# Re-ordering the hand-written stretch between the last filter lags and the first feed-forward block of an S4 + SwiGLU kernel

## The chip, the cores and the metric

The kernel runs on one core of one Trainium2 chip. The metric is the device time of one execution in microseconds (us). Below, PE is TensorE (matmuls), DVE is VectorE, ACT is ScalarE, POOL is GpSimd and SP is SyncE, which only issues DMAs here.

## The reference

Two layers, each a state-space block (S4) and then a feed-forward block (SwiGLU), on one sequence of 2048 rows with 512 channels; both layers use the same parameters:

```python
x = A_u
x = x + _A_ref(_layernorm(x), A_re, A_im, B_re, B_im, C_re, C_im, log_dt, Dskip)
x = x + _B_ref(_layernorm(x), w_gate, w_up, w_down)
...                                      # the same two lines once more

def _A_ref(u, ...):
    P = jnp.exp(logdA[:, :, None] * l)                      # 512 x 128 x 2048
    K = jnp.einsum("dn,dnl,dn->dl", Cc, P, dB).real         # one filter per channel
    y = irfft(rfft(pad(u)) * rfft(pad(K)))[:L]              # long convolution
    return y + u * Dskip

def _B_ref(x, w_gate, w_up, w_down):
    return (_silu(x @ w_gate) * (x @ w_up)) @ w_down        # 512 -> 1376 -> 512
```

## The kernel before

**Stages.** The sequence is cut into four blocks of 512 rows. A first stage makes the filter: the 512 channels are taken in eight chunks of 64; for each, VectorE and ScalarE build powers, TensorE sums them to the filter's lags (`lags`, 128 matmuls) and transforms them (`products`) into spectra. The first of the four spectrum blocks stays in SBUF (`w0r`), the others go to DRAM (`wdr`). In between, the first two row blocks of the layer-normed input are transformed as well (`direct`, and for the second row block `second`) and go to DRAM (`udr`).

The second stage works through the eight pairs (layer, row block) in the order of `SEQ`: convolution (`ssm_half`, for either half of the channels in four frequency steps) and feed-forward (`ffn`). Convolution of a pair and feed-forward of the pair before it run side by side: TensorE does the feed-forward's matmuls, VectorE mostly the spectra's products.

**A convolution step** of row block b: for each k up to b, multiply the input spectrum of block b-k with filter spectrum k (`yk`, then `t` and an add: lines 781 and 784), two instructions that combine real and imaginary parts into `y` (786, 787), eight inverse-transform matmuls `pi` (803), and then `combine`: a copy by ScalarE for frequencies 0 and 1 (753), two VectorE additions for 3 and 2 (761, 762). For k > 0 the spectra `w` and `uu` come by DMA from DRAM (777, 779). After the four steps two more groups of VectorE instructions make the output rows (818 to 822 and 827 to 834).

**The stretch that the change re-orders** lies between the two stages, about 240 to 315 us into the run. There the order of ScalarE's, VectorE's, TensorE's and GpSimd's instructions is that of the program, written by hand as a list of generator steps: `take(g, n)` issues the next n pieces of generator g. SyncE's order, and everything after this list, is set by a planner that runs the program on its own clock, with priorities (`tc.high_priority`). In the list are:

- `lags` of the last channel chunk, `spread_in` (a copy of the lags, line 507), `spread_pe` (32 matmuls, line 523, and a copy into `kt`, 525), `skip` (the direct term's addition on GpSimd, 503);
- `conv[0]` and `conv[1]`: the two halves of the first row block's convolution; `block1`: the second row block's;
- `scales`: eleven small VectorE instructions (344 to 356) that make the weights' scale factors, after the last `largest` (339);
- `split(hi, lo, load)`: the feed-forward weights as two fp16 parts, high part by ScalarE (664, for the down projection 689), low part by VectorE (669, 692), and their loads (660, 683, 685);
- `direct_size`: the largest direct term (ScalarE 192, VectorE 193);
- `first_parts`, `odd`, `rest`: the remaining spectra (580 and 531, with ScalarE 598 and 599 and VectorE 600); `spectra(6)`, third step: VectorE 563;
- `norm`: layer norm of the first 256 rows for the feed-forward (203 to 209, 848, transposes 850, 853, 855);
- `second(*sec[-1])`: the last transform of the second row block's input (16 matmuls, line 296, and a copy, 299).

Tiles share buffers by tag: a tile gets a buffer of its tag when the earlier tile in it is done with. The tag `w` has three buffers, for the `y` of the first convolutions (`yf`) and for the spectra `w`; `uu` has three; the PSUM tag `sml` has four.

Of the kernel before, what the change touches and what calls it, by code (L numbers as in the profile page):

```python
# [74 lines left out]
def kernel(ctx, tc, x, a_re, a_im, b_re, b_im, c_re, c_im, log_dt, d_skip,  # L75
# [12 lines left out]
    def tl(shape, name, tag, dt=F32):  # L88
        return sb.tile(shape, dt, name=name, tag=tag, bufs=BUFS[tag])
# [4 lines left out]
    def psml(shape, name):  # L94
        return ps.tile(shape, F32, name=name, tag="sml", bufs=4)
# [89 lines left out]
    dsk, th32 = tdk[0:1, 0], tdk[:, 1]  # L185
    nc.sync.dma_start(dsk, d_skip)
    dmax = sb.tile([1, 1], F32, name="dmax")

    def direct_size():

        da = tl([1, D], "da", "sg")
        A.activation(da, dsk, AF.Abs)
        V.tensor_reduce(dmax, da, axis=AX.X, op=OP.max)


# [304 lines left out]
    def skip(ch, kt, eng):  # L500

        k = kt[0:1, :, 0]
        eng.tensor_tensor(k, k, dsk[:, ch * DC:(ch + 1) * DC].rearrange("p (g d) -> p g d", g=4), OP.add)

    def spread_in(pk):
        ks = tl([P, 4, 16, 16], "ks", "nn")
        A.activation(ks, pk.rearrange("p d (c a) -> p a c d", a=4), AF.Copy)
        return ks
# [120 lines left out]
    def take(it, n):  # L629
        for _ in range(n):  # L630
            next(it, None)
# [70 lines left out]
    def inputs():  # L702

        for layer, b in SEQ:
            if layer == 0 and b < 2:
                if b == 0:
                    nc.sync.dma_start(u4, udr[0][0, 0].rearrange("q p c i d -> p q c i d"))
                for h in range(2):
                    for i, q in enumerate(QORD):
                        if b == 0:  # L710
                            u = u4[:, q]
                            for qn in (QORD[:3], QORD[3:], (), ())[i] if h else ():
                                nc.sync.dma_start(u4[:, qn], udr[0][0, 1, qn])
                        else:
# [23 lines left out]
    def ssm_half(layer, b, h):  # L738
# [3 lines left out]
        bb = {}  # L742
        if half and not yl2:
            yl2.append(tl([P, 2, 2, 2, HD], "yl2", "hf", F16))
        if (layer, b) == SEQ[1] and not yf2:
            t = tl([P, 2, 2, HD], "yf2", "hf")
            yf2.extend((t[:, 0], t[:, 1]))

        def combine(q, pi):
            if q < 2:  # L750
                pair = tl([P, 2, 2, HD], "bb", "bd") if h == 0 or not first else bb1[:, q]
# [9 lines left out]
                V.tensor_tensor(bb[q], s, pi, OP.subtract)  # L761
                V.tensor_tensor(s, s, pi, OP.add)

        late = []
        for s in range(4):
            hq, q, u = ahead.pop(0)
            nxt = next(spec, None)
            if nxt:
                ahead.append(nxt)
            yk = tl([P, NQ, 2, 2, DC], "yk", "y1")  # L770
            y = yc if half else yf2[s % 2] if (layer, b) == SEQ[1] else tl([P, 2, HD], "yf", "w")
            for k in range(b + 1):
                if k == 0:
                    w, uu = w0r[:, h, q], u
                else:
                    w = tl([P, NQ, 2, DC], "w", "w")
                    nc.sync.dma_start(w, wdr[k, h, q])
                    uu = tl([P, NQ, 2, DC], "uu", "uu")
                    nc.sync.dma_start(uu, udr[layer][b - k, h, q])
                t = tl([P, NQ, 2, 2, DC], "t", "t") if k else yk  # L780
                V.tensor_tensor(t, uu.unsqueeze(2).to_broadcast([P, NQ, 2, 2, DC]),  # L781
                                w.unsqueeze(3).to_broadcast([P, NQ, 2, 2, DC]), OP.mult)
                if k:
                    V.tensor_tensor(yk, yk, t, OP.add)  # L784
            yo = whole(y)
            V.tensor_tensor(yo[:, 0], yk[:, :, 0, 0], yk[:, :, 1, 1], OP.subtract)
            V.tensor_tensor(yo[:, 1], yk[:, :, 0, 1], yk[:, :, 1, 0], OP.add)
            if (layer, b, h, s) == (0, 1, 0, 0):
                yield
# [4 lines left out]
            pi = psml([P, 2, HD], "pi")  # L794
            with tc.high_priority(offset=0 if first else BOOST):
                for o in range(2):
                    if half:
                        terms = [(eih[:, q, 0 if i == o else 1 + o, le], yl[:, ly, i])
                                 for i in range(2) for le, ly in ((0, 0), (0, 1), (1, 0))]
                    else:  # L800
                        terms = [(ei[:, q, 0 if i == o else 1 + o], y[:, i]) for i in range(2)]
                    for k, (e, m) in enumerate(terms):
                        PE.matmul(pi[:, o], lhsT=e, rhs=m, start=k == 0, stop=k == len(terms) - 1)  # L803
            late.append((q, pi))
            if first and q < 2 or len(late) > 1:
                combine(*late.pop(-1 if first and q < 2 else 0))
            yield
        for l in late:
            combine(*l)
# [148 lines left out]
    with tc.manual_schedule(engines={mybir.EngineType.Activation, mybir.EngineType.DVE, mybir.EngineType.PE, mybir.EngineType.Pool}):  # L958
# [59 lines left out]
        def later(make):  # L1018

            yield from make()  # L1020
# [35 lines left out]
        def use(c, t):  # L1056

            box, kt, n = {}, kt2[:, c % 2], starts[c + 1]

            def copy():  # L1060
                box["ks"] = spread_in(box["pk"])
                if c < NCH - 2:
                    spread(c, box["ks"], kt)
            at(t, lambda: box.update(pk=lags(ts[c], gs[c])))
            at(t + 7.1, copy)
            if c == NCH - 2:
                at(t + 10.0, lambda: spread_pe(box["ks"], kt))
# [14 lines left out]
        def weights(n, t0, t1, t2, t3):  # L1082
# [15 lines left out]
            if t3:  # L1098
                at(t3, largest)

        starts = [0.0, 31.0, 62.0] + [93.0 + 28.0 * k for k in range(NCH)]
        for i in range(NCH - 1):
            t = starts[i]
# [18 lines left out]

        c, kts, tail = NCH - 1, (kt2[:, 0], kt2[:, 1]), {}
# [16 lines left out]
        def split(hi, lo, load=0):  # L1142
            for _ in range(load):
                loads.pop(0)()
            for _ in range(hi):
                his.pop(0)()
            for _ in range(lo):
                los.pop(0)()
# [61 lines left out]
        split(1, 0)  # L1210
        take(odd, 1)
        take(norm, 1)
# [65 lines left out]
```

## Time and profile before

| | |
|---|---|
| time, median of 3 runs | 1153.27 us (1152.6 to 1155.06) |
| the profiled execution | 1153.04 us, its span 1151.2 us |
| TensorE clock granted in it, mean | 0.993 |
| busy, share of the span | PE 95%, DVE 87%, ACT 52%, POOL 9% |
| instructions | 24402 |

The profile gives for every instruction its engine, its line in the kernel, its start and its length. "Idle before" is the time for which an engine had nothing to do before an instruction, with the instruction that released it. The profiled execution is 1.84 us longer than its span.

### The profile page before, as it was taken

What the parts mean: (1) busy time and instruction counts of PE and PEld (TensorE: products, weight loads), DVE (VectorE), ACT (ScalarE), POOL (GpSimd) and SP (SyncE); (2) the same over time, 40 slices, a digit from 0 to 9 for tenths busy, and PEclk for the clock granted to TensorE, in tenths of its full rate; (3) what the DMA queues carried; (4) which work ended last, traced back from release to release, by engine and by line L of the source; (5) the groups of instructions that cost most, each with busy time, mean ns of one, the idle gap of its engine ahead of it and who ended that gap; (6) DMA issues with size and microseconds to landing.
All of it is one profiled execution on the core that took longest, in us unless ns stands there. A gap on an engine that the chain in (4) does not pass through costs nothing.

```text
span 1151.2 us, 24402 instructions
## 1 busy us (share of the span) xinstructions
PE 1096.6 (95%) x9942; PEld 874.8 (76%) x9942; DVE 998.7 (87%) x1585; ACT 598.9 (52%) x1198; POOL 108.9 (9%) x163
## 2 busy tenths in 40 slices
PE   2989999998899999999999999999999999999998
PEld 1868888887776868686868777877768687776874
DVE  8999999988999899998999999989994999973221
ACT  6989998834554453567443534655424352334211
POOL 0112222210000110011010000110000100000000
PEclk9989999999999999999999999999999999999999
DMA  5367777867583355332355444334443155302000
GB/s 210 128 166 166 162 182 174 187 187 264 167 268 108 100 153 192 116 96 70 119 139 133 135 140 143 111 116 117 136 136 126 51 134 155 106 29 48 14 24 19
DMA packets 127314, 150.38 MB, mean 131 GB/s; under 512 B 50897, under 2 KB 75985, under 8 KB 127202
## 3 DMA queue, kind: packets, MB, share of 16 engines
q1 hardware_dynamic: 115298, 123.32, 35.1%
q0 software_dynamic: 11904, 25.50, 9.7%
q8 instruction: 78, 1.28, 0.4%
q14 instruction: 34, 0.28, 0.1%
HBM read 98.70 MB, written 33.82 MB: 115 GB/s over the span
## 4 chain that ended last, share of the span: by engine, by line
PE 40%; DVE 21%; issue 7%; DMA 4%; ACT 2%; POOL 1%; SPq 1%; DVEq 0%; ACTq 0%; POOLq 0%
PE pgu L916 7%; PE pgu L917 7%; PE pgu L919 7%; PE py L931 4%; PE py L932 4%; PE py L933 4%; PE pi L803 4%; DVE t L781 3%; DVE yk L784 3%; PE pf L280 2%; DVE z L228 2%; DVE yk L781 2%; DMA mix<-nn 2%; DVE sg L923 1%; DVE hl L925 1%
## 5 line engine op out<-in xcount | busy, mean ns | idle before, releaser
L916 PE MATMUL pgu<-mix,wsl 128*128 128x256 f16 x1280 | 299.2, 273 | 2.9 <-DVE sg L923 2.8
L917 PE MATMUL pgu<-mix,wsl 128*128 128x256 f16 x1280 | 298.8, 273 | 0.0
L919 PE MATMUL pgu<-mix,wsl 128*128 128x256 f16 x1280 | 195.6, 273 | 0.0
L917 PEld LDWEIGHTS <-wsl 128*128 128x128 f16 x1280 | 125.4, 98 | 19.8 <-issue 3.4
L931 PE MATMUL py<-wsl,hh 128*128 128x512 f16 (+1 forms) x352 | 133.5, 379 | 4.9 <-DVE xg L936 3.2
L916 PEld LDWEIGHTS <-wsl 128*128 128x128 f16 x1280 | 125.4, 98 | 16.0
L919 PEld LDWEIGHTS <-wsl 128*128 128x128 f16 x1280 | 125.5, 98 | 14.9
L933 PE MATMUL py<-wsl,hl 128*128 128x512 f16 (+1 forms) x352 | 133.4, 379 | 0.2 <-DVE hl L925 0.2
L922 ACT ACTIVATE sg<-pgu,sc 128x512 f32<-128x512 f32 x80 | 54.6, 683 | 129.1 <-PE pgu L919 126.2
L932 PE MATMUL py<-wsl,hh 128*128 128x512 f16 x320 | 121.3, 379 | 0.0
L781 DVE TENSOR_TENSOR t<-uu,w 128x1024 f32<-128x1024 f32 x96 | 116.8, 1217 | 0.2
L784 DVE TENSOR_TENSOR yk<-yk,t 128x1024 f32<-128x1024 f32 x96 | 116.8, 1217 | 0.2
L923 DVE SCALAR_TENSOR_TENSOR sg<-pgu,sc,sg 128x512 f32<-128x512 f32 x80 | 59.6, 745 | 52.5 <-ACT sg L922 52.3
L531 PE MATMUL pw<-kt,ek 128*128 128x256 f32 (+1 forms) x384 | 91.3, 375 | 0.0
L924 ACT ACTIVATE hh<-sg 128x512 f16<-128x512 f32 x80 | 50.1, 627 | 78.1 <-DVE sg L923 78.1
L803 PE MATMUL pi<-yl,mix 128*128 128x256 f16 x576 | 78.9, 272 | 1.6 <-ACT yl L792 1.2
L531 PEld LDWEIGHTS pw<-kt,ek 128*128 128x128 f32 x384 | 73.0, 194 | 8.4
L280 PE MATMUL pf<-z,eh 128*128 128x256 f16 x576 | 74.9, 273 | 0.6 <-DVE z L228 0.6
L781 DVE TENSOR_TENSOR yk<-u,w0r 128x1024 f32<-128x1024 f32 x56 | 68.1, 1217 | 0.8 <-ACT u L282 0.8
L925 DVE TENSOR_TENSOR hl<-sg,hh 128x512 f16<-128x512 f32 x80 | 54.8, 685 | 15.5 <-ACT hh L924 15.4
L496 PE MATMUL pk<-re,g 128*32 128x64 f32 x1024 | 65.1, 317 | 2.8 <-DMA g<-g 1.9
L932 PEld LDWEIGHTS <-hh 128*128 128x128 f16 (+1 forms) x352 | 34.5, 98 | 41.7 <-issue 5.9
(238 smaller groups left out, 2159.1 us busy)
## 6 DMA issues: line engine op xcount, KB each, us to landing
uu<-udr SPq DMA_DIRECT2D x96, 256.0 KB, 3.0
w<-wdr SPq DMA_DIRECT2D x96, 256.0 KB, 2.7
udr<-u POOLq DMA_DIRECT2D x32, 256.0 KB, 2.6
g<-g POOLq DMA_DIRECT2D x6, 1024.0 KB, 9.1
udr<-u SPq DMA_DIRECT2D x16, 256.0 KB, 3.0
n<-xdr SPq DMA_DIRECT2D x4, 1024.0 KB, 5.6
kdr<-ks SPq DMA_DIRECT2D x6, 512.0 KB, 2.8
kt<-kdr SPq DMA_DIRECT2D x24, 128.0 KB, 3.0
```

What stands on the lines that cost most here:

```text
L280: PE.matmul(pf[:, o], lhsT=e, rhs=m, start=k == 0, stop=k == len(terms) - 1)
L531: PE.matmul(pw[:, i], lhsT=e, rhs=kt[:, :, c + 4 * k0:4 * k1:4, :].rearrange("p g k d -> p k g d"), start=c == 0, stop=c == 3)
L781: V.tensor_tensor(t, uu.unsqueeze(2).to_broadcast([P, NQ, 2, 2, DC]), w.unsqueeze(3).to_broadcast([P, NQ, 2, 2, DC]), OP.mult)
L784: V.tensor_tensor(yk, yk, t, OP.add)
L803: PE.matmul(pi[:, o], lhsT=e, rhs=m, start=k == 0, stop=k == len(terms) - 1)
L916: PE.matmul(o, lhsT=wgu(wi, k, 0)[:, fs], rhs=nh[:, k], start=k == 0, stop=False)
L917: PE.matmul(o, lhsT=wgu(wi, k, 1)[:, fs], rhs=nh[:, k], start=False, stop=False)
L919: PE.matmul(o, lhsT=wgu(wi, k, 0)[:, fs], rhs=nlo[:, k], start=False, stop=k == 3)
L923: V.scalar_tensor_tensor(sg, pgu[:, 1], sc6[:, 4:5], sg, OP.mult, OP.mult)
L931: PE.matmul(py[:, r], lhsT=hh[:n, f, rc], rhs=wd(f, 0)[:n], start=f == 0, stop=False)
L932: PE.matmul(py[:, r], lhsT=hh[:n, f, rc], rhs=wd(f, 1)[:n], start=False, stop=False)
L933: PE.matmul(py[:, r], lhsT=hl[:n, f, rc], rhs=wd(f, 0)[:n], start=False, stop=f == FT - 1)
```

## The change

The list of the hand-written stretch gets another order, and around it these lines change:

```diff
     def direct_size():
-        da = tl([1, D], "da", "sg")
+        both = tl([1, D + DC], "da", "sg")
+        da = both[:, :D]
+        dlast.append(both[:, D:])
+        A.activation(dlast[0], dsk[:, D - DC:], AF.Copy)
         A.activation(da, dsk, AF.Abs)
+        yield
         V.tensor_reduce(dmax, da, axis=AX.X, op=OP.max)
...
-            y = yc if half else yf2[s % 2] if (layer, b) == SEQ[1] else tl([P, 2, HD], "yf", "w")
+            y = yc if half else yf2[s % 2] if (layer, b, h + s > 0) == (*SEQ[1], True) else tl([P, 2, HD], "yf", "w")
...
+            if ahead_two and s == 0:
+                q, u = QORD[0], tl([P, NQ, 2, DC], "u", "u")
+                nc.sync.dma_start(u, udr[0][1, 0, q])
...
+            made.append((q, y, yl))
+            if ahead_two and s == 0:
+                yield
+                continue
+            while made:
+                if ahead_two and s == 1:
+                    yield
+                inverse(*made.pop(0))
...
+                if c == NCH - 2:
+                    tail["sp"] = sp
+                    ats = ats[:2]
```

`ahead_two` holds for layer 0, row block 1, first half; `inverse` is the old code of the eight `pi` matmuls and `combine`, now a function; the last lines take the third and fourth piece of `spectra(6)` out of the plan. The list itself (lines that stay are given where the order needs them):

```diff
+        take(conv[0], 1)
+        take(tail["sp"], 2)
+        while tops:
+            tops.pop(0)()
+        scales()
+        split(1, 0)
+        size = direct_size()
+        next(size)
         ks = spread_in(pk)
...
+        last = second(*sec[-1])
         take(conv[0], 1)
+        split(0, 1)
+        split(0, 0, 1)
+        take(size, 1)
         spread_pe(ks, kts[1])
         skip(c, kts[1], G)
         take(conv[0], 1)
-        while tops:
-            tops.pop(0)()
-        scales()
+        block1 = ssm(0, 1)
+        take(block1, 1)
+        first_parts(c, 0)
         split(1, 0)
-        first_parts(c, 0)
-        take(conv[0], 1)
-        split(1, 1)
-        split(0, 0, 1)
         first_parts(c - 1, 3)
         split(1, 0)
         take(conv[0], 1)
         first_parts(c - 1, 1)
         split(1, 0)
+        take(last, 2)
+        split(0, 1)
+        split(0, 0, 1)
         take(conv[1], 1)
         first_parts(c, 2)
         take(conv[1], 1)
-        split(0, 1)
-        split(0, 0, 1)
...
         take(odd, 2)
         take(conv[1], 1)
-        direct_size()
-        block1 = ssm(0, 1)
         take(norm, 1)
         take(rest, 2)
         take(odd, 1)
+        take(odd, 2)
         take(norm, 1)
         take(block1, 1)
         take(rest, 1)
-        take(odd, 2)
...
         sizes(c, kts[1], ks)
-        take(second(*sec[-1]), 2)
```

So the scale factors, the first high part and the largest direct term are issued ahead of the copy of the last lags; the first convolution step is issued ahead of the last spectrum's addition; the second row block's first two steps (VectorE's five instructions each, without their inverse transforms) come after the first convolution's third step and after the norm's second piece; the last transform of the second row block's input comes after the third `first_parts`. `skip` reads a copy of the last 64 direct terms; the tile with the originals shares its buffer with `t`, so a `t` now waits for `direct_size` alone. The `y` of that row block's first step takes a buffer of tag `w`.

More of the change, by code (lines that the diff above doesn't have):

```diff
@@ L187 @@
     dmax = sb.tile([1, 1], F32, name="dmax")
+    dlast = []
     def direct_size():
-        da = tl([1, D], "da", "sg")
+        both = tl([1, D + DC], "da", "sg")
+        da = both[:, :D]
+        dlast.append(both[:, D:])
+        A.activation(dlast[0], dsk[:, D - DC:], AF.Copy)
         A.activation(da, dsk, AF.Abs)
+        yield
         V.tensor_reduce(dmax, da, axis=AX.X, op=OP.max)
@@ L502, in skip @@
         k = kt[0:1, :, 0]
-        eng.tensor_tensor(k, k, dsk[:, ch * DC:(ch + 1) * DC].rearrange("p (g d) -> p g d", g=4), OP.add)
+        d = dlast[0] if ch == NCH - 1 else dsk[:, ch * DC:(ch + 1) * DC]
+        eng.tensor_tensor(k, k, d.rearrange("p (g d) -> p g d", g=4), OP.add)
     def spread_in(pk):
@@ L713, in inputs @@
                                 nc.sync.dma_start(u4[:, qn], udr[0][0, 1, qn])
+                        elif h + i == 0:
+                            continue
                         else:
@@ L744, in ssm_half @@
             yl2.append(tl([P, 2, 2, 2, HD], "yl2", "hf", F16))
-        if (layer, b) == SEQ[1] and not yf2:
-            t = tl([P, 2, 2, HD], "yf2", "hf")
-            yf2.extend((t[:, 0], t[:, 1]))
         def combine(q, pi):
@@ L762, in combine, with inverse @@
                 V.tensor_tensor(s, s, pi, OP.add)
-        late = []
-        for s in range(4):
[L766 to L769, printed above, removed]
+        late, made = [], []
+        ahead_two = (layer, b, h) == (0, 1, 0)
+        def inverse(q, y, yl):
+            pi = psml([P, 2, HD], "pi")
+            with tc.high_priority(offset=0 if first else BOOST):
+                for o in range(2):
+                    if half:
+                        terms = [(eih[:, q, 0 if i == o else 1 + o, le], yl[:, ly, i])
+                                 for i in range(2) for le, ly in ((0, 0), (0, 1), (1, 0))]
+                    else:
+                        terms = [(ei[:, q, 0 if i == o else 1 + o], y[:, i]) for i in range(2)]
+                    for k, (e, m) in enumerate(terms):
+                        PE.matmul(pi[:, o], lhsT=e, rhs=m, start=k == 0, stop=k == len(terms) - 1)
+            late.append((q, pi))
+            if first and q < 2 or len(late) > 1:
+                combine(*late.pop(-1 if first and q < 2 else 0))
+        for s in range(4):
+            if ahead_two and s == 0:
+                q, u = QORD[0], tl([P, NQ, 2, DC], "u", "u")
+                nc.sync.dma_start(u, udr[0][1, 0, q])
+            else:
+                hq, q, u = ahead.pop(0)
+                nxt = next(spec, None)
+                if nxt:
+                    ahead.append(nxt)
             yk = tl([P, NQ, 2, 2, DC], "yk", "y1")
-            y = yc if half else yf2[s % 2] if (layer, b) == SEQ[1] else tl([P, 2, HD], "yf", "w")
+            if (layer, b, h + s > 0) == (*SEQ[1], True) and not yf2:
+                t = tl([P, 2, 2, HD], "yf2", "hf")
+                yf2.extend((t[:, 0], t[:, 1]))
+            y = yc if half else yf2[s % 2] if (layer, b, h + s > 0) == (*SEQ[1], True) else tl([P, 2, HD], "yf", "w")
             for k in range(b + 1):
@@ L787, in ssm_half @@
             V.tensor_tensor(yo[:, 1], yk[:, :, 0, 1], yk[:, :, 1, 0], OP.add)
-            if (layer, b, h, s) == (0, 1, 0, 0):
-                yield
+            yl = None
             if half:
@@ L793, in ssm_half @@
                 stt(yl[:, 1], y, sy[:, 0:1], yl[:, 0], OP.subtract)
[L794 to L806, printed above, removed]
+            made.append((q, y, yl))
+            if ahead_two and s == 0:
+                yield
+                continue
+            while made:
+                if ahead_two and s == 1:
+                    yield
+                inverse(*made.pop(0))
             yield
@@ L1099, in weights @@
                 at(t3, largest)
+        tail = {}
         starts = [0.0, 31.0, 62.0] + [93.0 + 28.0 * k for k in range(NCH)]
@@ L1121 @@
                 plan.pop(0)[2]()
-        c, kts, tail = NCH - 1, (kt2[:, 0], kt2[:, 1]), {}
+        c, kts = NCH - 1, (kt2[:, 0], kt2[:, 1])
         xs, eh, yl2, yf2 = [None] * 3, [], [], []
```

## The prediction

> **What bounds the kernel now.** I read the page first, then the waits of TensorE by stage, then the timelines of all engines between 245 and 330 us, where the edits lie.
>
> ```profile
> PE 1096.6 (95%) x9942; PEld 874.8 (76%) x9942; DVE 998.7 (87%) x1585; ACT 598.9 (52%) x1198; POOL 108.9 (9%) x163
> 256.95:313.43 56.48, 47.17 (x293) 42.50 (x289) 50.21 (x85) 27.90 (x58) 1.65 (x2) 0.97 0.61 200
> 340.00:1151.20 811.20, 798.92 (x6685) 614.72 (x6683) 679.23 (x1130) 349.40 (x677) 53.31 (x68) 1.00 0.36 106
> PE pt L850 <- ACT nn L848: 4.8, 1, 4.8
> PE pi L803 <- DVE yf L786: 4.5, 2, 2.7
> ```
>
> The second and third row are stretches (length, then busy time of PE, weight loads, DVE, ACT, POOL, then the granted clock, the DMA share and GB/s). After 340 us TensorE is idle for 12.3 of 811 us while VectorE idles for 132: the rest is TensorE's, and whatever the edited stretch gives or takes at the first feed-forward matmul is carried to the end nearly one for one. In the edited stretch TensorE idles for 9.3 us, each time for VectorE's work (the waits for `nn` hang on the norm's VectorE part); one more wait, at 324 us, is shown further below. VectorE in turn has two waits of its own:
>
> ```profile
> 249.50 0.97 DVE L563 TENSOR_TENSOR wo<-pw,wo 128x768 f32<-128x768 f32 x1 [2.89 <-ACT w0r L559]
> 250.37 1.22 DVE L781 TENSOR_TENSOR yk<-mix,w0r 128x1024 f32<-128x1024 f32 x1
> 252.44 1.23 DVE L781 TENSOR_TENSOR yk<-mix,w0r 128x1024 f32<-128x1024 f32 x1
> 256.61 1.22 DVE L781 TENSOR_TENSOR yk<-mix,w0r 128x1024 f32<-128x1024 f32 x1
> 263.26 1.78 DVE L669 SCALAR_TENSOR_TENSOR wsl<-st,sc,wsl 128x688 f16<-128x688 f32 x2 [4.64 <-ACT wsl L664]
> 256.95 1.99 PE L803 MATMUL pi<-yf,mix 128*128 128x256 f32 x8
> 258.87 1.93 PE L523 MATMUL kp<-ks,ident 128*32 128x256 f32 x32
> 260.74 1.99 PE L803 MATMUL pi<-yf,mix 128*128 128x256 f32 x8
> 262.57 0.55 PE L580 MATMUL pw<-kt,ef 128*128 128x64 f32 x4
> 257.16 1.02 ACT L507 ACTIVATE ks<-pk 128x1024 f32<-128x1024 f32 x1 [7.70 <-PE pk L497]
> 258.98 0.60 ACT L753 ACTIVATE bb<-pi 128x512 f32<-128x512 f32 x1 [0.79 <-PE pi L803]
> 261.79 1.43 ACT L664 ACTIVATE wsl<-st,sc 128x1376 f16<-128x1376 f32 x1
> ```
>
> **VectorE's two waits.** The first convolution step (250.37 to 252.44: 2.07 us) now fills most of the wait of 2.89; the spectrum's addition still waits for ScalarE until 249.5. The gain of 2.0 does not last. ScalarE works in the order of the list, and there the copy of `pi` (258.98) now stands ahead of the first high part, and that `pi` still comes behind the last lags, at 256.95. So the high part starts at 258.98 + 0.5 instead of 261.79, and the low part on VectorE at about 260.8 instead of 263.26: 2.4 earlier. But the third convolution step (2.05, at 256.61), which lay ahead of it, now lies behind it. When both are done VectorE is at 263.26 + 1.78 = 265.0 before and at 260.8 + 1.8 + 2.05 = 264.7 now. Of 7.5 us of waits, 0.3 are won. The size of the direct terms stays ahead of the norm in both orders and drops out; its tile shares a buffer with the spectrum's sum, whose stores have 9 us to land by then.
>
> On TensorE the copy of the lags (`ks`, 257.16 before) now stands behind that `pi` copy, the high part (1.35 to the next) and the direct terms (0.5): it ends at 262.3. The second `pi` is moved ahead of `kp`, which then waits from 260.7 to 262.2. TensorE reaches 264.1 with work that it had done at 262.57: 1.5 lost. GpSimd's `skip` is 3.3 us later too, but its reader waits for TensorE until 266.9, beyond it.
>
> **The second row block's first step.** It is five VectorE instructions:
>
> ```profile
> 290.11 0.67 DVE L193 TENSOR_REDUCE dmax<-da 1x1 f32<-1x512 f32 x1
> 294.73 1.22 DVE L781 TENSOR_TENSOR yk<-u,w0r 128x1024 f32<-128x1024 f32 x1
> 299.15 0.55 DVE L600 TENSOR_TENSOR wos<-pw,wos 128x384 f32<-128x384 f32 x1
> 258.62 0.85 SPq L660 DMA_DIRECT2D wsl<-in_B_w_up_dram  x1
> 259.52 1.39 SPq L232 DMA_DIRECT2D xg<-in_A_u_dram  x1
> 261.01 1.90 SPq L713 DMA_DIRECT2D mix<-udr  x1
> mix<-udr SPq DMA_DIRECT2D x1, 256.0 KB, 10.3
> wsl<-in_B_w_up_dram SPq DMA_DIRECT2D x1, 688.0 KB, 9.3
> 262.00:264.00 2.00, 2.00 (x18) 1.92 (x16) 0.74 (x1) 1.22 (x1) 0.29 (x1) 1.00 1.07 395
> ```
>
> The step takes 294.73 to 299.15, 4.4 us, and now lies at about 265, ahead of the fourth convolution step, not in a wait. Its `uu` and `u` need no late buffer. Its `w` does: the tag's three buffers belong to the first convolution steps, so its load can start only when the first or second `pi` is done, at 258.9 or 260.7. That is inside the burst of weight loads (395 GB/s, DMA share 1.07). VectorE wants `w` at 264.7 + 0.6 (the direct terms' reduction, 0.67, overlapping a little) + 1.1 = 266.3 or so. If the load goes where the 256 KB of `mix` go now (issued at 261.01, 10.3 us to land), it lands at 271.3: a stall of 5.0. If SyncE issues it ahead of the second `xg` load (259.52), it follows the 688 KB load of 258.62 that took 9.3 (267.9), plus 0.7 for 256 KB at 395 GB/s: 268.6, a stall of 2.3. Behind one more weight load (688 KB, 1.8 at that rate) it would be 6.8; with a buffer free earlier, 0. I take 5.0, the row of the same size at the same place in SyncE's queue. Behind the waiting product on VectorE stands the fourth convolution step, and TensorE waits for that.
>
> The `y` of this step keeps one of the three `w` buffers until after the list, so the later steps share two. Each then needs the `pi` two steps back, which is done by 1 us or more by the same count: 0, and up to 1.8 (one `pi`) if not.
>
> **The norm and the first feed-forward matmul.**
>
> ```profile
> 279.51 1.99 PE L803 MATMUL pi<-yf,mix 128*128 128x256 f32 x8 [2.73 <-DVE yf L786]
> 295.25 1.82 PE L850 MATMUL pt<-ident,nn 128*128 128x128 f32 x8 [4.79 <-ACT nn L848]
> 299.15 0.49 PE L531 MATMUL pw<-kt,ef 128*128 128x192 f32 x2
> 300.45 0.49 PE L531 MATMUL pw<-kt,ef 128*128 128x192 f32 x2
> 308.25 0.59 PE L296 MATMUL pf<-n,ef 128*128 128x256 f32 x2
> 308.68 1.89 PE L803 MATMUL pi<-yf,mix 128*128 128x256 f32 x8
> 313.43 0.27 PE L916 MATMUL pgu<-mix,wsl 128*128 128x256 f16 x1
> 278.00:280.00 2.00, 0.49 (x2) 0.45 (x3) 1.97 (x4) 0.00 (x0) 0.00 (x0) 1.00 0.03 11
> 296.00:298.00 2.00, 2.00 (x10) 2.00 (x9) 1.97 (x2) 0.89 (x1) 0.00 (x0) 0.50 0.94 271
> ```
>
> From the first low part to the norm VectorE waits for nothing before (the row of 263.26 is its last wait there), so the norm, and the transposes `pt` that TensorE waits for, come later by what is put ahead of them: 4.4 - 0.3 + stall = 4.1 + stall. After `pt` TensorE has less left. Gone ahead are the last transform (308.25 to 313.43 without the `pi`, 3.45) and one `odd` spectrum (two groups of 1.3, by 299.15 to 300.45: 2.6); its copy and DMA go at a time with little traffic (0.03 at 278) and cost nothing, or 0.5 on ScalarE without that cover. The wait before `pt` falls from 4.8 to some 1.6, because TensorE arrives later. With it goes the half clock of 296 to 298: between 295.25 and 308.25 are 1.6 + 8 x 1.3 = 12.0 us of work in 13.0, so 1.0. Sum: -3.45 - 2.6 - 1.0 + 0.2 (a PSUM buffer) + 4.1 = -2.7, plus the stall. The second step in the list takes the first one's old place on VectorE; its `pi`, 1.75, also goes ahead of the feed-forward, but is work that would follow anyway. With a stall of 5.0 the feed-forward starts 2.3 later in its own terms; with 2.3, 0.4 earlier.
>
> The stall makes one more TensorE wait, at about 271, of 1.2 + 5.0 us: it is through its own work at 270.4, and the fourth step's `y` is made at 266.3 + 3.2 + 2.05 = 271.6 plus the stall. The wait of 4.79 is followed by a clock of 0.50, the one of 2.73 by 1.00 (278 to 280); so expect 0.50 there. Some 3.4 us at half speed cost 1.7, which the next two waits for VectorE (0.5 and 1.9 by the same count) swallow: 0. [...]
>
> **After the start.**
>
> ```profile
> 310.20 0.93 SPq L683 DMA_DIRECT2D st<-in_B_w_down_dram  x2
> 315.25 4.40 ACT L689 ACTIVATE wsl<-st,sc 128x512 f16<-128x512 f32 x7 [1.02 <-DMA st<-in_B_w_down_dram]
> 322.82 1.28 ACT L922 ACT_TABLE_LOAD   x1
> 326.85 0.37 PE L916 MATMUL pgu<-mix,wsl 128*128 128x256 f16 x1 [2.78 <-DVE sg L923]
> 326.00:328.00 2.00, 1.15 (x6) 0.84 (x6) 2.00 (x5) 1.17 (x2) 0.00 (x0) 0.54 1.55 305
> ```
>
> TensorE fills its two `pgu` buffers in 324.07 - 313.43 = 10.6 us and waits 2.78 for them, because ScalarE does eleven high parts of the down projection (from 315.25) ahead of the first Silu (322.82). With 1.35 for the half clock behind it the hole is worth 4.1. Now those weights are loaded when the last output rows of the first block are made (310.20), which comes 4.1 - 0.3 + stall = 8.8 later, so the high parts begin at 324.1; the feed-forward starts at 313.4 + 2.3 + 1.75 = 317.5 and fills up at 328.1. If the planner keeps all eleven ahead, TensorE goes on at 326.85 + 8.8 = 335.7, a wait of 7.6. If it puts Silu first, there is none. Its clock put all eleven ahead although the first `pgu` was done (318.7, half of the 10.6 us on) after five of them at 0.63; now that `pgu` (322.8) comes ahead of the first, so a part should slip behind. I take the middle, 3.8: 1.0 more than now.
>
> **Sum.** 1153.04 (this execution, 0.23 under the median of 1153.27) + 2.3 + 1.0 = 1156.3 us.
>
> **Rivals.** (1) Faster: the planner puts Silu ahead of the down projection's high parts. The hole goes (-4.1), and with a stall of 5.0 the time is 1153.04 + 2.3 - 4.1 = 1151.2, with 2.3 it is 1148.5. It is a clear gain from a stall of 4.5 down. For it: that `pgu` is ready first; against: the order now. (2) The hole grows to 7.6: 1153.04 + 2.3 + 4.8 = 1160.1. (3) The load of `w` comes early and the change does what it says: -2.7, and the middle hole: 1151.3; against it stand the three buffers. (4) The terms cancel: a stall of 2.3 with the middle hole gives 1153.04 - 0.4 + 1.0 = 1153.6.
>
> **How the numbers follow.** A stall of 5.0 gets 0.6, of 2.3 0.3, none 0.1; no hole 0.3, the middle 0.4, the full one 0.3. The planner also orders the 811 us behind anew, where 12.3 idle us can shrink little and grow more; I spread each case by 2 us, more of it upward. Within 0.2%, 2.3 us, a measurement of this kernel can't tell from no change: 1151.0 to 1155.6. Slower then gets 0.49: rival 2 (0.18), three quarters of the forecast's case (0.18 of 0.24), the full hole with the shorter stall (0.09, at 1157.4) and 0.04 from the edges of rivals 3 and 4. Faster gets 0.27: rival 1 with the shorter stalls (0.12), half of it with 5.0 (0.09 of 0.18), and 0.06 from those edges. No change gets the rest, 0.24. The range is 1149 to 1161: it takes in rivals 1 and 2, and leaves out the early load with no hole and what the planner could add to rival 2.
>
> **What would show it.** VectorE's wait for the first low part stays, at about 255 to 260.8. The first product with `w` waits for a DMA until 268 to 271, and a TensorE wait of 3 to 6 us with a clock of 0.50 follows. `pt` waits under 2 us. The first Silu's place among the eleven high parts tells the hole. I am wrong if `w` is there by 266, if the first low part starts well before 260, or if the time differs while the first feed-forward matmul has not moved.

## The result, and the profile after

| | before | after |
|---|---|---|
| time, median of 4 runs each on one chip | 1152.93 us (1151.99 to 1155.06) | 1170.95 us (1169.69 to 1171.87) |
| ratio to before, 95% interval | | 1.015 [1.013, 1.0169] |
| profiled execution, its span | 1153.04, 1151.2 us | 1169.69, 1167.9 us |
| first feed-forward matmul (PE `pgu`) | 313.43 us | 313.62 us |

The change makes the kernel 18 us slower; forecast were 3.3 us. The two profiled executions differ by 16.65 us, and the first feed-forward matmul, which the prediction used as its clock, has not moved. So the profile is read in two parts, cut at 352 us, behind the first row block's first feed-forward columns. First the page's busy row of after, then two stretches of it (length, then busy time of PE, weight loads, DVE, ACT, POOL, then clock, DMA share, GB/s):

```profile
PE 1102.7 (94%) x9942; PEld 878.3 (75%) x9942; DVE 998.9 (86%) x1585; ACT 600.0 (51%) x1199; POOL 108.4 (9%) x163
244.00:352.00 108.00, 91.58 (x834) 81.37 (x833) 90.85 (x154) 46.42 (x91) 4.85 (x5) 0.94 0.67 209
352.00:1167.90 815.90, 795.33 (x6608) 610.04 (x6606) 672.80 (x1121) 350.82 (x676) 51.35 (x67) 1.00 0.36 105
```

The same two stretches of before:

```profile
244.00:352.00 108.00, 95.92 (x880) 85.30 (x879) 96.53 (x163) 49.34 (x94) 3.36 (x5) 0.97 0.70 215
352.00:1151.20 799.20, 786.92 (x6561) 604.15 (x6559) 667.26 (x1112) 346.70 (x672) 53.15 (x67) 1.00 0.36 106
```

Up to 352 us TensorE idles for 108 - 91.58 = 16.4 us instead of 12.1. Behind it, where the change edits nothing, it idles for 20.6 instead of 12.3. The time lost at half clock from 244 us on (by the trace's clock records, less the idle time in them) is 6.9 us instead of 3.1, 3.2 of it behind 352 us, where before loses none. These are 4.3 + 8.3 + 3.8 = 16.4 us. Ahead of 244 us after idles for 2.1 us less and loses 0.8 us more at half clock, so 15.1 of the 16.65 us are accounted for.

**Up to 352 us.** TensorE's waits between 244 and 352 us, and VectorE's between 236 and 300 us (engine, line, what it waited for: sum, times, longest):

```profile
PE pi L781 <- DVE yf L814: 9.7, 3, 8.7
PE pgu L905 <- DVE sg L945: 2.3, 1, 2.3
PE kp L529 <- ACT ks L513: 1.9, 1, 1.9
PE pt L872 <- ACT nn L870: 1.6, 1, 1.6
PE pgu L938 <- DVE sg L945: 0.9, 1, 0.9
```

```profile
DVE t L809 <- DMA w<-wdr: 7.6, 1, 7.6
DVE wsl L675 <- ACT wsl L670: 6.3, 1, 6.3
DVE wo L569 <- ACT w0r L565: 1.1, 1, 1.1
```

The product with `w` waits 7.6 us for its load, and TensorE 8.7 us for the step queued behind that product. The timeline of after shows where the load stood (start, length, engine; SPq is SyncE issuing):

```profile
259.55 1.39 SPq L237 DMA_DIRECT2D xg<-in_A_u_dram  x1
260.90 1.78 DVE L675 SCALAR_TENSOR_TENSOR wsl<-st,sc,wsl 128x688 f16<-128x688 f32 x2 [6.29 <-ACT wsl L670]
262.74 0.37 SPq L666 DMA_DIRECT2D st<-in_B_w_gate_dram  x1
264.43 0.34 SPq L719 DMA_DIRECT2D mix<-udr  x1
264.99 0.34 SPq L805 DMA_DIRECT2D w<-wdr  x1
274.01 1.23 DVE L809 TENSOR_TENSOR t<-uu,w 128x1024 f32<-128x1024 f32 x1 [7.56 <-DMA w<-wdr]
```

SyncE issues `w` at 264.99: behind the second `xg` load, one more weight load, which waits for the first low part, and the load of `mix`, whose buffer comes free only with the third convolution step's product (263.19 on VectorE). SyncE's own waits between 258 and 266 us show both:

```profile
SPq L666 <- DVE wsl L675: 1.8, 1, 1.8
SPq L719 <- DVE yk L809: 1.2, 1, 1.2
```

The load of `w` lands 8.9 us after its issue. The granted clock during and behind TensorE's wait, as two stretches of after:

```profile
270.00:280.00 10.00, 1.32 (x7) 1.04 (x6) 5.71 (x8) 2.04 (x3) 0.00 (x0) 0.65 0.44 157
280.00:290.00 10.00, 10.00 (x49) 8.75 (x48) 9.55 (x17) 2.31 (x3) 0.00 (x0) 0.84 0.45 118
```

**Behind 352 us.** No single wait is long. TensorE's largest there in after:

```profile
PE py L953 <- DVE xg L958: 6.7, 5, 3.5
PE pi L781 <- ACT yl L819: 3.1, 1, 3.1
PE pgu L938 <- DVE sg L914: 1.7, 1, 1.7
```

In before the longest of them is 1.2. These instructions are not the change's, but their order is new: everything behind the hand-written list is laid out by the planner, and of VectorE's last 900 instructions 304 stand elsewhere than in before (how this was counted stands ahead of the table below). What that does is seen best at the longest wait. The timeline of after around 820 us:

```profile
779.42 1.23 DVE L809 TENSOR_TENSOR yk<-u,w0r 128x1024 f32<-128x1024 f32 x1 [4.73 <-ACT u L287]
817.30 0.69 DVE L891 TENSOR_TENSOR nn<-nn 128x512 f16<-128x512 f32 x1 [2.02 <-DMA mix<-nn]
817.91 1.22 DVE L809 TENSOR_TENSOR t<-uu,w 128x1024 f32<-128x1024 f32 x1
820.31 1.22 DVE L812 TENSOR_TENSOR yk<-yk,t 128x1024 f32<-128x1024 f32 x1
822.12 0.75 DVE L958 SCALAR_TENSOR_TENSOR xg<-py,sc,xg 128x512 f32<-128x512 f32 x1
822.91 0.59 PE L953 MATMUL py<-wsl,hh 128*128 128x512 f16 x1 [3.46 <-DVE xg L958]
```

and the same piece of work in before:

```profile
814.09 0.68 DVE L869 TENSOR_TENSOR nn<-nn 128x512 f16<-128x512 f32 x1
814.69 0.74 DVE L228 SCALAR_TENSOR_TENSOR yl<-mix,sy,yl 128x512 f16<-128x512 f32 x1
815.35 0.74 DVE L936 SCALAR_TENSOR_TENSOR xg<-py,sc,xg 128x512 f32<-128x512 f32 x1
```

TensorE's next down projection (`py`) needs the `xg` sum on VectorE. In before only the short `nn` and `yl` stand between it and the convolution product ahead of them, and neither VectorE nor TensorE waits there. In after VectorE first stands still for a DMA (2.02 us) and then does a convolution product and the addition to it, with smaller things between: `xg` runs 4.8 us after the stall's end. Ahead of 779 us VectorE lost another 4.73 us waiting for ScalarE's copy `u`. In before its waits for `u` sum to 0.8 us, in after to 8.6.

### The profile page after: what moved, and what is told of

It is laid out like the page before. It is cut to its first block, busy times and chain, and to the rows that moved or that the text cites. A ratio compares the mean times of both kernels' runs of the same rounds, so it can differ in the third digit from the quotient of the medians.

```text
span 1167.9 us, 24410 instructions
## 1 busy us (share of the span) xinstructions
PE 1102.7 (94%) x9942; PEld 878.3 (75%) x9942; DVE 998.9 (86%) x1585; ACT 600.0 (51%) x1199; POOL 108.4 (9%) x163
## 4 chain that ended last, share of the span: by engine, by line
PE 38%; DVE 27%; issue 5%; DMA 3%; ACT 1%; POOL 1%; SPq 0%; DVEq 0%; ACTq 0%; POOLq 0%
PE pgu L938 6%; PE pgu L939 6%; PE pgu L941 6%; DVE t L809 5%; PE py L953 4%; PE py L954 4%; PE py L955 4%; DVE yk L812 4%; PE pf L285 3%; PE pi L781 3%; DVE yk L809 3%; DVE z L233 2%; DVE sg L945 2%; DVE hl L947 1%; DVE bt L233 1%
## 5 line engine op out<-in xcount | busy, mean ns | idle before, releaser
L287 ACT ACTIVATE u<-pf 128x512 f32<-128x512 f32 x48 | 28.4, 592 | 76.2 <-PE pf L285 76.2
```

## The experiments

Four theories, and a fifth from e10 on. **A**: the stall for `w` is the whole loss. **B**: about half is the stall, about half the planner's other order of the rest. **C**: the re-ordered front costs. **D**: the rest suffers from what it is handed (lateness, buffers still held), whatever its order. **E**: the earlier scale that re-orders the rest in e5, e6 and e8 is worth its gain by itself. Each ratio below is to before, run in the same rounds on the same chip, with its 95% interval. Kernels of different rounds ran on different chips, where before's median was 1152.93 to 1153.81 us, so differences between two kernels hold to about 1 us. "Moved" is the number of VectorE's last 900 instructions that stand elsewhere than in before, counted in the order that the planner laid out, before the run; it depends on how two orders are lined up. Compared place by place in the traces, 538 of the 900 differ from before in after and e1, 540 in e3, 549 in e11, 119 in e4, 110 in e5 and e6, 102 in e2, e7 and e9, and none in e8 and e10; kernels with the same count here have the same order. The idle time is TensorE's behind 352 us.

| kernel | time, us (range) | ratio | moved | idle |
|---|---|---|---|---|
| after | 1170.95 (1169.69 to 1171.87) | 1.015 [1.013, 1.0169] | 304 | 20.6 |
| e1_w_early | 1162.69 (1162.14 to 1164.26) | 1.0083 [1.0068, 1.0099] | 304 | 20.6 |
| e2_steps_back | 1148.42 (1147.17 to 1148.65) | 0.9955 [0.994, 0.997] | 66 | 12.4 |
| e3_steps_only | 1172.37 (1171.7 to 1175.59) | 1.0172 [1.0149, 1.0194] | 382 | 18.5 |
| e4_last_only | 1156.26 (1155.22 to 1156.98) | 1.0021 [1.0012, 1.003] | 97 | 14.2 |
| e5_replan | 1158.86 (1157.01 to 1161.6) | 1.0043 [1.0029, 1.0056] | 105 | 12.6 |
| e6_w_early_replan | 1151.12 (1149.58 to 1152.02) | 0.998 [0.997, 0.999] | 105 | 12.3 |
| e7_front | 1150.72 (1149.19 to 1152.19) | 0.9978 [0.9966, 0.999] | 66 | 12.1 |
| e8_all_mended | 1146.4 (1145.23 to 1147.73) | 0.9936 [0.9916, 0.9956] | 0 | 12.2 |
| e9_front_replan | 1147.74 (1146.82 to 1150.41) | 0.9948 [0.9931, 0.9966] | 66 | 12.9 |
| e10_replan_alone | 1154.83 (1154.15 to 1156.39) | 1.0009 [1.0, 1.0019] | 0 | 13.4 |
| e11_steps_other_order | 1158.56 (1157.17 to 1163.65) | 1.0046 [1.0031, 1.0061] | 446 | 19.8 |

**e1_w_early.** After, with the early step's `w` in a buffer of the tag `u`, whose buffers are free earlier.

```diff
-                    w = tl([P, NQ, 2, DC], "w", "w")
+                    w = tl([P, NQ, 2, DC], "w", "u" if ahead_two and s == 0 else "w")
```

> The changed kernel, with the first step's w in a buffer of tag u, free early, so that its load is issued before the burst of weight loads; the planner's order of VectorE and ScalarE behind the list is the same as in the changed kernel, instruction for instruction. Theory A (the stall is the whole loss: 7.6 us of VectorE, the half clock behind it and the lateness that follows): VectorE's wait for w goes, TensorE's wait of 8.7 falls to about 1.2, and the time comes back to 1150 to 1154 us. Theory B (about half of the loss is the planner's other order of the 800 us behind the list): the stall and its half clock go, some 8 to 9 us, and the time stays at 1160 to 1164 us, with TensorE waits of about 16 us after 340 us as in the changed kernel (7 before).

The wait for `w` is gone, and 8.3 us of time with it (1170.95 to 1162.69); the first feed-forward matmul comes 7.8 us earlier, at 305.8. VectorE's order of the rest is after's, and TensorE's idle time there is after's too:

```profile
352.00:1160.30 808.30, 787.73 (x6550) 603.95 (x6548) 665.04 (x1108) 347.69 (x671) 51.02 (x67) 1.00 0.35 104
```

808.30 - 787.73 is 20.6 again. A falls: without the stall the kernel is still 0.83% slower than before.

**e2_steps_back.** After, with the second row block's first step issued only where before has it.

```diff
         take(conv[0], 1)
-        block1 = ssm(0, 1)
-        take(block1, 1)
         first_parts(c, 0)
...
         take(norm, 1)
+        block1 = ssm(0, 1)
         take(block1, 1)
```

> The changed kernel without the two early steps of the second row block: that block's first step is issued where it was before; all other edits stay. Behind the list 66 of the last 900 VectorE instructions stand in another order than before (304 in the changed kernel). Both theories: no stall, so near the kernel before; by the prediction's own terms 1149 to 1152 us (last transform ahead of the norm -3.5, half clock before the transposes -1.0, copy of the lags later +1.5). If the front edits were what costs (theory C), it stays above 1160 us.

Faster than before by 0.45% (0.6 us under the range expected), at the same idle time behind 352 us as before. The rest of the change costs nothing: C falls. The early steps carry the whole loss: without them the stall and most of the other order are gone.

**e3_steps_only.** Before, with the two early steps and what they need (the direct terms in two pieces, the copy of the last of them), nothing else.

```diff
+        size = direct_size()
+        next(size)
...
+        block1 = ssm(0, 1)
+        take(block1, 1)
...
-        direct_size()
-        block1 = ssm(0, 1)
+        take(size, 1)
```

> The kernel before, with the two early steps alone (and what they need: the direct terms' first piece ahead of spread_pe, the copy of the last 64 terms, the first step's y in tag w). 382 of the last 900 VectorE instructions behind the list stand in another order. Theory A: the stall for w is there again, 5 to 8 us, and the time is 1158 to 1163. Theory B: stall and other order, 1164 to 1173. Theory C: 1153 to 1156.

The whole loss and more, with the stall at its largest, as VectorE's and TensorE's waits between 244 and 352 us show:

```profile
DVE t L809 <- DMA w<-wdr: 12.3, 1, 12.3
```

```profile
PE pi L781 <- DVE yf L814: 14.0, 3, 11.0
```

VectorE comes to the step earlier here than in after (its product before it is at 258.87 instead of 265.23), and the load, issued at 263.46, lands at about 272. The early steps alone, with their late load and an order of the rest that is new again (382 moved, 18.5 us of idle time), make the loss.

**e4_last_only.** Before, with the last transform of the input between the first parts.

```diff
+        last = second(*sec[-1])
...
         split(1, 0)
+        take(last, 2)
...
-        take(second(*sec[-1]), 2)
```

> The kernel before, with the last transform of the second row block's input alone moved to the place behind the third first_parts, into a stretch where TensorE waits for VectorE. 97 of the last 900 VectorE instructions behind the list stand in another order. The prediction priced it at -3.5 us at the first feed-forward matmul. Theory A: 1149 to 1150 us. Theory B: the same at the first feed-forward matmul, but the end can be anywhere from 1148 to 1156, as the planner's other order gives or takes.

A small loss, 0.3 us above the range that B allowed. The transform's move does bring the first feed-forward matmul 2.8 us forward, to 310.6 (the prediction priced it at 3.5), but TensorE gives it back before 352 us, where the first Silu's results come late, and behind it, where 97 moved instructions go with 14.2 us of idle time instead of 12.3. TensorE's waits between 244 and 352 us:

```profile
PE pgu L916 <- DVE sg L923: 6.0, 3, 4.5
PE pt L850 <- ACT nn L848: 4.8, 1, 4.8
```

**e5_replan.** After, and the two lines that hand the planner the product's scale come ahead of the first convolution. The work is the same; the planner lays out the rest in another order, with 105 instead of 304 moved.

```diff
     for i, lb in enumerate(SEQ):
+        if i == 0:
+            take(pscale, 100)
         if i + 1 < len(SEQ):
             take(ssm(*SEQ[i + 1]) if i else block1, 100)
-        if i == 0:
-            take(pscale, 100)
```

> The changed kernel, with one edit behind the list: the few instructions of product_scale are issued ahead of the rest of block1 instead of behind it. The list and all its waits stay; the planner's order behind it is another: 105 of the last 900 VectorE instructions stand elsewhere than in the kernel before, against 304 in the changed kernel. Theory B (the planner's order of the rest costs about as much as the stall): TensorE's waits after 350 us fall from 16 to 7 or 8 us without a half clock there, and the time from 1171 to 1158 to 1162. Theory D (the rest suffers because the list hands it a later VectorE or other buffers, whatever the order): 1168 to 1172.

The stall is still there, and so is the first feed-forward matmul (313.7); 12.1 us are gone. Behind 352 us TensorE idles for 8.0 us less, and the 3.2 us that after loses there at half clock (0.57 granted from 600 to 604 us and from 822 to 826), behind two of its waits, are gone too, by a mean granted clock of 0.991 instead of 0.988:

```profile
352.00:1156.20 804.20, 791.62 (x6605) 608.99 (x6602) 672.26 (x1118) 349.09 (x676) 50.42 (x67) 1.00 0.35 106
```

**e6_w_early_replan.** The edits of e1 and e5 together.

> The kernel of e1_w_early (no stall for w), with the same one edit behind the list as e5_replan. Theory B: neither stall nor bad order, 1149 to 1153 us, so about 10 less than e1_w_early's 1162.7. Theory D: 1160 to 1163.

The two add up: 11.6 us less than e1, 7.7 less than e5, and the kernel is now a little faster than before.

```profile
352.00:1148.20 796.20, 783.87 (x6547) 602.76 (x6545) 664.51 (x1101) 346.48 (x671) 50.32 (x67) 1.00 0.36 106
```

So far B; D falls in its strong form, since the same state handed over gives 20.6 or 12.3 us of idle time by the order alone.

**e7_front.** e2, and the first convolution step behind the copy of the lags, so that scales, first high part and size come ahead of it.

```diff
-        take(conv[0], 1)
         take(tail["sp"], 2)
...
         ks = spread_in(pk)
+        take(conv[0], 1)
```

> The kernel of e2_steps_back, with the first convolution step moved behind the copy of the lags: the last spectrum's addition, scales, first high part and direct terms then come first on VectorE and ScalarE, ahead of the pi copy that waits for the lags. VectorE's order behind the list is that of e2_steps_back, instruction for instruction. By the prediction's terms VectorE's wait of 6.3 us for the first high part goes for one of 2.9 for the spectrum, kp's wait of 1.85 goes, and the next TensorE waits (0.5, 0.9, 1.6) shrink: 2 to 4 us less than e2_steps_back, 1144 to 1147. If the front order is worth nothing: 1148.

Missed by 3.7 us. Ahead of the norm the front does what was expected of it: the wait before `kp` is gone and the norm's transposes come 3.3 us earlier than in e2 (293.7 against 297.0). The first feed-forward matmul does not follow, at 306.1 against 303.4: eight `pi` matmuls and sixteen of the spectra's stand ahead of it here that e2 has behind it, and a half clock lies between (0.59 granted from 295.5 to 299 us). And the planner puts one high part of the down projection ahead of the first Silu, and it waits for its weights, as ScalarE's waits and TensorE's show:

```profile
ACT wsl L695 <- DMA st<-in_B_w_down_dram: 7.7, 1, 7.7
```

```profile
PE pgu L938 <- DVE sg L945: 5.6, 1, 5.6
```

In e2 no high part stands there. That these two take back the front's gain is likely, not shown. Half clock for 6.8 us follows (0.50 granted from 323 to 329).

**e8_all_mended.** After with e1's buffer, e7's front and e5's two lines. VectorE's order of the rest is then exactly that of before.

> All edits of the change with three mends: w of the first step in an early buffer (e1), scales and first high part ahead of the first convolution step (e7), product_scale ahead of block1's rest (e5). VectorE's last 900 instructions then stand in the order of the kernel before. Theory B: no loss is left, 1144 to 1150 us. Theory D: the early steps still cost some 10 us, 1156 to 1162.

The lowest median of all, 0.64% under before. The early step runs without a wait, as the timeline shows, and the granted clock is 1.00 from 244 to 352 us and in the stretch behind:

```profile
261.32 1.23 DVE L809 TENSOR_TENSOR yk<-u,w0r 128x1024 f32<-128x1024 f32 x1
262.46 1.22 DVE L809 TENSOR_TENSOR t<-uu,w 128x1024 f32<-128x1024 f32 x1
352.00:1145.50 793.50, 781.35 (x6535) 601.64 (x6533) 662.58 (x1097) 345.91 (x671) 52.99 (x67) 1.00 0.35 106
```

**e9_front_replan.** e7 with e5's two lines; the first Silu now stands ahead of all high parts.

> The kernel of e7_front (front edits, none of the two early steps) with the product's scale listed ahead of the direct terms' first block in the final list, so that ScalarE's first Silu stands ahead of all eleven high parts of the down projection. Question: did the wait of 5.6 us before the first Silu, with 6.8 us at a low clock behind it, take back what the front edits won in e7 (1150.7)? If so, 1144 to 1147, first feed-forward matmul at 303 to 307, no wait of over 3 us between 315 and 340. If the front edits cost something elsewhere (theory C), about 1150 still.

3.0 us less than e7 by the medians, 0.7 above the range expected. That the hole before the first Silu made the 3 us is likely, not shown: the profiled execution is the longest of its five (1150.41 us), and in it the wait of 5.6 is gone but one of 4.3 us stands at 336.9, and the mean granted clock is 0.992 (e7: 0.993). Against e8 (1146.4) the difference is 1.3 us, with overlapping intervals and another order of the rest (66 moved against none), so no gain of the early steps is shown.

**e10_replan_alone.** Before with e5's two lines; VectorE's order does not change.

> The kernel before with nothing but the product's scale listed earlier, as in e5, e6 and e8. VectorE's order of the rest is the one of before. Theory B (what e5 and e6 won they won by the order of the rest): this alone changes nothing or little, 1150 to 1155, at most the hole of 2.78 us before the first Silu with its 1.35 of half clock goes. Rival E: the earlier scale itself is worth 8 to 12 us wherever it is put; then 1141 to 1145.

Nothing is won: 1.0009 [1.0, 1.0019]. E falls: the earlier scale is worth nothing by itself, and what e5 and e6 won is the order's. The hole before the first Silu, which the expectation allowed to go, stayed (2.7 us).

**e11_steps_other_order.** e8 without e5's two lines.

> The kernel of e8_all_mended (1146.4) without the earlier product's scale: 446 of VectorE's last 900 instructions then stand in another order than before. Early w, front order and both early steps as in e8. Theory B: the other order costs again, 1152 to 1162, with TensorE idle after 352 us over 10 us instead of 7.6. Rival D (the rest suffers from what is handed over, not from its order): within 2 us of 1146.4.

12.2 us slower than e8. The front is not quite e8's: from 244 to 352 us TensorE idles for 9.0 us against 9.6, but loses 1.7 us at half clock (0.56 granted from 296 to 299 us) against none, and the first feed-forward matmul comes at 308.0 against 304.7, with eight `pi` matmuls more ahead of it. The idle time is where B puts it:

```profile
352.00:1155.50 803.50, 783.74 (x6542) 602.44 (x6539) 661.23 (x1100) 347.25 (x671) 51.10 (x67) 1.00 0.35 105
```

19.8 us against 12.2, and 1.7 us at half clock (0.50 granted from 474 to 477 us) against none. Three pairs that differ by the two lines alone, and so by the order of the rest (after and e5, e1 and e6, e11 and e8), differ by 12.1, 11.6 and 12.2 us; the 1.7 us of half clock in e11's front are part of the last. Over all kernels the idle time goes with the number moved: 12.1 to 14.2 us up to 105, 18.5 to 20.6 from 304 on; within either group it does not follow the number. The longest wait for `u` is 4.7 us in after and e1 and 4.9 in e11; in e5 and e8 VectorE's waits for `u` sum to 0.6 and 0.8. Which of the moved instructions matter was not tried one by one, so the timeline around 820 us above shows how such an order costs at one place, not that this place makes the most of it. Nor is it shown why one order of two lines makes the planner keep before's sequence and the other not.

## Why the prediction was wrong

**The term that failed: carrying the stretch to the end.** The prediction said that what the stretch gives is carried "nearly one for one", and spread each case by 2 us because the planner orders the 811 us behind it anew. The carrying holds where the order holds: up to 352 us e8 won 5.6 us (idle time 9.6 instead of 12.1, half clock 0 instead of 3.1), and its profiled execution is 5.7 us shorter; e6, with nearly before's order, won 2.8 and is 3.0 shorter. The spread was mis-sized: the new order costs about 12 us by the three pairs, in after 8.0 of it TensorE's idle time and 3.2 half clock. The prediction read TensorE's 12 idle us there as small, and not as the result of one particular order. That VectorE's short sums for TensorE (`xg`, `sg`, `yl`) come just in time between convolution products of 1.2 us is what the rows of before at 815 us show at one place; that it is so throughout was not tried. The range ended at 1161, and no case in it had a dearer rest.

**The stall: right in kind, too small.** 5.0 was taken, with 6.8 as the upper end; it measured 7.56. VectorE came to the product at 266.45 (said: 266.3). The load was issued at 264.99, not at 261.01. Ahead of it stood the second `xg` (counted), one more weight load (the bound of 6.8) and the load of `mix`, which was not counted. SyncE's waits for VectorE in between, 1.8 us for the weight load and 1.2 for `mix`, were not counted either; the product that `mix` waits for comes later by the change (263.19 instead of 256.61). TensorE's wait was 8.68 (said: 1.2 + 5.0). By e1 the stall costs 7.8 us at the first feed-forward matmul and 8.3 of time. The half clock behind it came, for 10.24 us (272.9 to 283.1) instead of some 3.4 (before's two periods there last 3.41 us), and was swallowed nearly as said: 7.8 us for a stall of 7.56.

**The front: right.** The first low part starts at 260.90 (said: about 260.8), behind a wait of 6.3; VectorE's two waits sum to 7.4 us instead of 7.5, so 0.1 is won (said: 0.3). `ks` ends at 262.4 (said: 262.3) and `kp` waits 1.85 (said: 1.5 lost). `pt` waits 1.6 (said: some 1.6). What the prediction didn't weigh is that the first convolution step, listed first, holds up the high part: with it behind, in e8, the first low part starts at 257.0 and `kp` doesn't wait. In time no gain is shown: e9 against e2, with the same 66 moved, is 1147.7 to 1148.4.

**The hole before Silu: right in size, with luck.** Forecast were 3.8 us of waiting, 1.0 more than before, so 5.1 with half clock; after has 0.93 at 339.9 and 2.29 at 347.6, and half of the 3.4 us at half clock behind, 4.9. But the middle was taken between all high parts ahead of the first Silu and none. One stands ahead of it in after and waits 6.2 us for its weights; the others come behind it, and the two waits are for later Silus that stand behind them. The working also takes the 0.3 off twice where it moves the high parts by 8.8 us (4.1 + 5.0 is 9.1); nothing else turns on that.

**The sum up to 352 us.** With the measured stall the prediction's terms give 2.3 + 1.0 + 2.56 = 5.9 us. TensorE lost 4.3 us in idle time and 0.6 at half clock there: 4.9. Without a stall (rival 3) it gave 1151.3; e6, which is that with a rest as good as before's, measured 1151.1. So the sum of the stretch was predicted within about 1 us, though not where the first feed-forward matmul lies in it (next paragraph), and the miss of 14.6 us is nearly all the order (about 12) and the longer stall (2.6).

**The sign that was named.** "If the time differs while the first feed-forward matmul has not moved" was listed as what would prove the argument wrong, and it is what happened: 313.62 against 313.43 (said: 317.5). That matmul was a poor clock besides: between 257 us and it TensorE did 267 matmuls instead of 293. Eight `pi` and sixteen of the spectra's, which before has ahead of it, come behind it, so it stood still while the work behind it fell back. The prediction had put one more `pi` ahead of it.

## What to carry to other kernels

Where a planner lays out the work behind an edited stretch, an edit moves instructions far away: look at the order of the rest first, and price a changed order by itself (here about 12 us for a third of VectorE's last 900 instructions), apart from the edit. An edit can be judged once the order of the rest is held; two lines in another order did that here (1170.95 to 1158.86 us), and with an early buffer for the load and another front 1.5% slower became 0.64% faster. Work pulled ahead needs its loads pulled ahead: follow the load through the issuing queue, with what each entry ahead of it waits for (here 1.8 and 1.2 us, for a stall of 7.56), and give it a buffer that is free by then.

## What the runs showed of the hardware

The half-clock periods in the clock records of before and after last 3.41 us or two or three times that, apart from the last, which begins at 1148.8 and 1167.2 us and runs past the kernel's end. Before has one of 6.83 us from 70.2 us on and two of 3.41, from 295.4 and 326.2; after has one of 6.83 from 71.5 on, one of 10.24 from 272.9, and three of 3.41, from 348.0, 600.6 and 822.5. The length of a single wait did not tell whether the clock fell: it fell in e7 after a wait of 1.63 us (0.59 from 295.5 to 299), in e11 after one of 1.96 and in after behind one of 3.15 (0.57 from 600 to 604), and stayed at 1.00 after one of 3.53 in e11 and of 3.2 in e8 (338 to 342). Rows of e11, first the two waits, then the clock behind them:

```profile
473.22 0.38 PE L953 MATMUL py<-wsl,hh 128*128 128x512 f16 x1 [1.96 <-DVE xg L958]
602.11 0.27 PE L938 MATMUL pgu<-mix,wsl 128*128 128x256 f16 x1 [3.53 <-DVE xf L958]
474.00:477.00 3.00, 3.00 (x9) 1.04 (x8) 3.00 (x6) 0.63 (x1) 0.00 (x0) 0.50 0.63 208
602.00:606.00 4.00, 3.89 (x36) 3.49 (x36) 4.00 (x8) 1.08 (x2) 0.00 (x0) 1.00 0.61 213
```

The same wait was followed by either clock. The 1.63 us ahead of the norm's transposes, behind which the clock fell in e7, stand in e9 with a clock of 1.00 behind them, and in e2 as 1.6 us in a stretch at 1.00 (240 to 320). The wait in e7 and in e9, and the clock behind it in e7, then in e9:

```profile
293.66 1.36 PE L872 MATMUL pt<-ident,nn 128*128 128x128 f32 x8 [1.63 <-ACT nn L870]
294.34 1.36 PE L872 MATMUL pt<-ident,nn 128*128 128x128 f32 x8 [1.63 <-ACT nn L870]
295.50:299.00 3.50, 3.50 (x15) 3.50 (x14) 3.44 (x5) 3.30 (x11) 0.00 (x0) 0.59 1.04 341
295.50:299.00 3.50, 3.50 (x24) 3.50 (x23) 3.43 (x6) 3.26 (x9) 0.00 (x0) 1.00 1.05 341
```

The longest wait after 244 us had half clock in it or behind it in before, after and e7: 4.79 us in before (0.50 from 296 to 298), 8.68 in after (0.65 from 270 to 280) and 5.6 in e7 (0.50 from 323 to 329). What decided it for the shorter waits above was not shown.
